# Retention, a dense MoE layer and eight routed experts on one core: weight conversion moved in time, and the expert norms one step later

## The chip, the cores and the metric

The kernel runs on one core of a Trainium2 chip. The metric is device time in microseconds (us) of one execution, the median of three runs. Engine names are those of the profile: PE (matrix engine), PEld (its weight loads), DVE (vector engine), ACT (scalar engine), POOL (GpSimd), SP (the queue from which nearly all transfers are issued).

## The reference

Three layers follow each other (float32 in and out):

```python
scores = q @ k.T / 8                 # 4 batches, 8 heads, 576 positions, 64 wide
ret = scores * D                     # D[i,j] = gamma_h ** (i-j) for i >= j, else 0
x = (ret @ v)                        # -> 2304 tokens x 512
h = x @ w_in;  g = h / (1 + exp(-1.702 h));  x = g @ w_out      # 512 -> 2048 -> 512
xn = x / (|x| + 1e-6);  en = emb / (|emb| + 1e-6)               # emb: 8 experts x 512
probs = softmax(xn @ en.T / tau);  e = argmax                   # one expert per token
out = probs[e] * (relu(x @ w1[e]) @ w2[e])                      # 512 -> 1024 -> 512
```

In this kernel the dense weights `w_in` and `w_out` come in as pairs of 32-bit words, that is as 64-bit numbers, and the chip rebuilds a float from each pair. The weights of the experts are plain floats.

## The kernel before, in words

Every product of the two feed-forward layers is made of three passes, high times high, high times low, low times high, where high is the rounded value that PE takes and low is the rest. So a weight "unit" (128 rows of the hidden layer, 1024 columns, both layers together) is a tile of a high and a low half.

**Attention** (`attention_`, L207). Sixteen pairs of heads, each of five chunks of positions, so 80 chunks; two neighbouring pairs alternate, so each pair starts five chunks after the one before. For a chunk, PE makes the scores two chunks ahead (L269, L272 for the short last chunk), DVE multiplies them by the decay table (`pr`, L274), PE makes the running state (L296), ACT copies it with a factor to `ends` (L298), and PE makes the output (L312 reads `ends`, L316 reads `pr`). POOL prepares the queries and the decayed keys of a pair two pairs ahead (`prep`, L276: L281, L284, L287). The rows of a pair are loaded into one of five buffers as soon as the pair that used it is done (`load`, L222); behind three of these loads, chosen by `WD_AT`, a dense weight unit is loaded too (L372).

**Conversion** (`convert`, L138) is a generator that issues the work for the 16 dense units, a piece at a time. For unit u: ACT takes the magnitude of the upper word (`magnitude`, L146), DVE clamps it (L159) and shifts it (L161), puts in the sign (L169) and the low bits (L171); ACT then rounds it to the high half (`high`, L149), and DVE takes the low half (`low`, L153). Each `yield` names a cost in us. ACT's two operations are not issued on the spot: they are put into `later` and issued at the next `flush()`, or when the next piece needs them. The intermediate words have two buffers, taken in turn.

**Pull** (L687) issues pieces from the list `bg` of generators until the costs reach the number given; what is overdrawn is taken off the next time. In the attention it is called after each chunk from the 53rd on with 0.36; in the dense layer once for each step. A `STOP` makes it go on with the next generator, at a charge of 0.7.

**Dense layer.** Six blocks of 384 tokens. Blocks 0 and 1 go together, unit by unit: step i is block i mod 2 with unit i // 2 (32 steps). Blocks 2 to 5 follow with 16 steps each. In step i, `dense1(i)` makes the hidden rows (PE, 12 products, L410) and the activation (`swish`, L425: ACT tanh, DVE product L434, ACT high part, then in blocks 0 and 1 `flush()` and `pull`, then DVE low part L439), and `dense2(i - 2)` adds to the outputs (PE, 9 products, L421). So the conversion of units 2 to 15 lies in the 32 steps of blocks 0 and 1, in DVE's queue between the product and the low part of each step.

**Routing.** When a block is done its outputs are copied (`evac_x`) and `dots_dve` (L500) is put into `bg`: 24 dot products of rows with the experts' vectors (L507), then `route` (L523): a chain of small DVE operations up to `oh` (L547, the chosen expert as ones and zeros), two STOPs, a PE product with `oh` that counts the places (`rk`, L554), STOP, the scatter, STOP, a store. At the end of each of the blocks 2 to 4 what is left in `bg` is issued at once (L747). `route` multiplies by `etab`, which `prep_emb` (L476) makes from the expert vectors: eight ACT squares (L479), a POOL square root (L474), three small DVE operations (L483 to L485). It is put into `bg` in step 27, after the conversion has been drained there.

**Tiles and queues.** All engines and SP work in program order. A tile of a tag with n buffers waits until the tile n before it under the same tag has been read. The tag "stg" holds the two conversion words and later `x0s`, the tokens of block 2 and on; the tag "tab" holds two of the query tiles of the attention, then the two halves of the experts' vectors (`en`), then gathered rows.

Of the kernel before, what the change touches and what calls it, by code (L numbers as in the profile page):

```python
# [13 lines left out]
I32 = mybir.dt.int32  # L14
AF = mybir.ActivationFunctionType
ALU = mybir.AluOpType

P = 128
# [5 lines left out]
KD = D // P  # L24
F1 = 2048
NF1 = F1 // P
# [13 lines left out]
WARM = 34  # L40
HOLD = NF1 - LAG - 1 - KD
STOP = 1000.0
WD_AT = (9, 12, 15)
NWD = 3
NBUF, NQ = 5, 4
HELD = NBUF + NPAIR + 4
# [16 lines left out]
def retention_moe_kernel(  # L63
# [14 lines left out]
    pool = ctx.enter_context(tc.tile_pool(name="pool", bufs=1))  # L78
# [3 lines left out]
    PE, ACT, DVE, POOL, SP = nc.tensor, nc.scalar, nc.vector, nc.gpsimd, nc.sync  # L82
# [27 lines left out]
    def new_unit(u):  # L110
        units[u] = unit_tile(f"unit{u}", [P, 2, 1024], F32R, HELD + u)
        return units[u]

    stg = {}

    def load_wd(u):

        t = unit_tile(f"wd{u}", [P, 2048], I32, HELD + u)
        stg["d", u] = t.rearrange("p (n two) -> p n two", two=2)
        SP.dma_start(t, wd[u].bitcast(I32))  # L120
# [3 lines left out]
    later = {}  # L124
    due = []

    def load_due():

        if st.get("loaded"):
            while due:  # L130
                load_wd(due.pop(0))

    def flush(*keys):
        for k in keys or list(later):
            if k in later:
                later.pop(k)()

    def convert():  # L138

        words = [pool.tile([P, 1024], I32, tag="stg", bufs=2, name=f"ca{k}") for k in range(2)]  # L140

        def word(u):
            return words[u % 2]

        def magnitude(u):
            ACT.activation(word(u).bitcast(F32), stg["d", u][:, :, 1].bitcast(F32), AF.Abs)  # L146

        def high(u):
            ACT.copy(new_unit(u)[:, 0, :], word(u).bitcast(F32))  # L149

        def low(u):
            flush(("high", u))
            DVE.tensor_tensor(units[u][:, 1, :], word(u).bitcast(F32), units[u][:, 0, :].bitcast(F32), ALU.subtract)  # L153

        magnitude(0)
        for u in range(NF1):
            a = word(u)
            flush(("mag", u))
            DVE.tensor_scalar(a.bitcast(F32), a.bitcast(F32), 2.0**-15, CLAMP_HI, ALU.max, ALU.min)  # L159
            yield 0.67  # L160
            DVE.tensor_scalar(a, a, 3, 0x3FFFFFF8, ALU.logical_shift_left, ALU.bitwise_and)  # L161
            yield 0.67
            if u:
                low(u - 1)
                yield 1.22
            if u + 1 < NF1:
                later["mag", u + 1] = lambda u=u: magnitude(u + 1)
            d = stg.pop(("d", u))
            DVE.scalar_tensor_tensor(a, d[:, :, 1], -0x40000000, a, ALU.bitwise_and, ALU.bitwise_or)  # L169
            yield 1.22  # L170
            DVE.scalar_tensor_tensor(a, d[:, :, 0], 29, a, ALU.logical_shift_right, ALU.bitwise_or)  # L171
            if u + NWD < NF1:
                due.append(u + NWD)
                load_due()
            later["high", u] = lambda u=u: high(u)
            yield 1.22
        low(u)
        yield 0.1
# [23 lines left out]
    def attention():  # L202
        psum = tc.tile_pool(name="psum_a", bufs=1, space=bass.MemoryType.PSUM, reuse_waits="tile")
        with psum as psum:
            yield from attention_(psum)

    def attention_(psum):  # L207
# [14 lines left out]
        def load(bp):  # L222
            t = row[bp % NBUF]
            b, pair = divmod(bp, NPAIR)
            if bp:
                SP.dma_start(t, att[bp])
            else:
                for j in range(2):
                    r = slice(64 * j, 64 * j + 64)
                    SP.dma_start(qz[0][r, S * j : S * j + NCH * P], att[bp, r, AQ:])  # L230
                ACT.dma_start(t[:, :AK], att[bp, :, :AK])
            if b == 0:
                SP.dma_start(tb[:, bp], tab[:, bp])
            if bp == 0:
                ACT.dma_start(t[:, AK:AQ], att[bp, :, AK:AQ])
            if pair == 0:
                SP.dma_start(tl[b % 2], tails[b])
# [121 lines left out]
        for i, (bp, ch) in enumerate(steps):  # L359
# [9 lines left out]
            if ch == NCH:  # L369
                if bp + NBUF < NBP:  # L370
                    load(bp + NBUF)
                if bp + NBUF in WD_AT:  # L372
                    load_wd(WD_AT.index(bp + NBUF))
                if bp + NBUF + 1 == NBP:
# [13 lines left out]
    def x0_tile(blk):  # L388
        return pool.tile([P, 2, KD, TB], F32R, tag="big", bufs=2, name=f"x0_{blk}")
# [7 lines left out]
    def split_x0(blk):  # L397
        x0[blk] = x0_tile(blk)
        for k in range(2):
            t = x0s.pop((blk, k))  # L400
            hi, lo = (x0[blk][:, j, 2 * k : 2 * k + 2, :] for j in range(2))
            ACT.copy(hi, t)  # L402
            (POOL if blk > 2 and k else DVE).tensor_tensor(lo, t, hi.bitcast(F32), ALU.subtract)  # L403
# [21 lines left out]
    def swish(h, name, early=False, kept=None, work=None):  # L425
        th = pool.tile([P, TB], F32, tag="th", bufs=2, name=f"{name}t")
        if kept:
            hi, lo = kept
        else:
            hi = pool.tile([P, TB], F32R, tag="g", bufs=6, name=f"{name}h")  # L430
            lo = pool.tile([P, TB], F32R, tag="g", bufs=6, name=f"{name}l")
        ACT.activation(th, h, AF.Tanh, scale=0.851)
        g = th if early else h
        DVE.scalar_tensor_tensor(g, th, 1.0, h, ALU.add, ALU.mult)  # L434
        ACT.copy(hi, g)
        if work:
            flush()
            work()
        DVE.tensor_tensor(lo, g, hi.bitcast(F32), ALU.subtract)  # L439
        return hi, lo  # L440
# [32 lines left out]
    def sqrt_(o, i):  # L473
        POOL.tensor_tensor(o, i, c[:, CHALF : CHALF + 1].to_broadcast(i.shape), ALU.pow)  # L474

    def prep_emb():  # L476
        for e in range(E):
            junk = pool.tile([P, 512], F32, tag="cvb", bufs=1, name=f"ej{e}")
            ACT.activation(junk, en[e // 4][:, e % 4, :], AF.Square, accum_out=scr[:, e : e + 1])  # L479
            yield 0.3  # L480
        nrm = small("enrm", E)
        sqrt_(nrm, scr[:, :E])
        DVE.tensor_scalar_add(nrm, nrm, 1e-6)  # L483
        DVE.tensor_scalar(nrm, nrm, scr[:, 15:16], None, ALU.mult)
        DVE.reciprocal(etab, nrm)  # L485
        yield 0.4
# [198 lines left out]
    bg, debt = [], [0.0]  # L685

    def pull(us):  # L687

        k = 0
        us += debt.pop()  # L690
        while us > 0 and k < len(bg):
            cost = next(bg[k], None)
            if cost is None:
                bg.pop(k)
            elif cost == STOP:
                k += 1
                us -= 0.7
            else:
                us -= cost
        debt.append(min(us, 0.0))  # L700

    bg.append(convert())
    for i, _ in enumerate(attention()):
        if i > 52:
            flush()
            pull(0.36)
    psum = ctx.enter_context(tc.tile_pool(name="psum", bufs=1, space=bass.MemoryType.PSUM, reuse_waits="tile"))

    def fill_slots():
# [9 lines left out]
    gs, outs = {}, {}  # L719
# [3 lines left out]
    kept = []  # L723
# [5 lines left out]
    def dense1(i):  # L729
        blk, f = steps[i]  # L730
        k = f - HOLD if blk == NB - 1 else -1
        if k == 0:
            kept.append(x0_tile("k"))
        h = layer1(f, x0[blk], TB, f"h{i}", [(dc, a, b) for dc in range(KD) for a, b in ((0, 0), (0, 1), (1, 0))])
        gs[blk, f] = swish(h, f"g{i}", blk < 3, [kept[0][:, j, k, :] for j in range(2)] if 0 <= k < KD else None, (lambda: pull(2.5)) if blk < 2 else None)

    def dense2(i):
        blk, f = steps[i]
# [111 lines left out]
    for i in range(nd - 1):  # L850
        blk, f = steps[i]
        dense1(i)
        if blk < 2:
            if f > 3:
                next(fill, None)
            if blk == 1 and f < NPAIR:
                SP.dma_start(x0d[:, f, :], x0f.pop(f))
            if (blk, f) == (1, NF1 - 3):
                while bg:
                    pull(STOP)  # L860
                load_emb()
                bg.append(prep_emb())
                load_x0(2)
            if (blk, f) == (0, NF1 - 1):
                split_x0(2)
        else:
            pull(2.6 if blk == 2 else 2.0)
            if blk < NB - 1 and f == 0:
                load_x0(blk + 1)
            if blk < NB - 1 and f == 6:  # L870
                split_x0(blk + 1)
        if i >= LAG:
            dense2(i - LAG)
            u = i - LAG - (nd - NF1)
            if u == 0:
                load_we(0)
                load_we(1)
            if 0 <= u < HOLD:
                split_we(u)
# [33 lines left out]
    for i in range(ne + LAG):  # L913
        e, f = divmod(i, NF2)
# [93 lines left out]
```

## Time and profile before

| | us |
|---|---|
| median of three runs | 794.12 (793.67 to 795.09) |
| the profiled execution | 794.88 |
| its span | 793.1 |
| PE busy | 758.5 (96%) |
| DVE busy | 455.9 (57%) |
| ACT busy | 304.4 (38%) |
| POOL busy | 225.8 (28%) |

The attention lies at 0 to 79 us of the span, blocks 0 and 1 at 79 to 230, blocks 2 to 5 to about 510, the experts behind them. In a timeline a row is the start, the duration, the engine, the line, and in brackets how long the engine had been idle and what ended that. The duration of a row of several instructions runs from the first start to the last end. DVE's rows overlap by a tenth of a us or so at their ends, so the distance from start to start is what one costs.

### The profile page before, as it was taken

To read this page: it belongs to the slowest core of one execution; us is meant where nothing else is said; L and a number is where in the kernel's file an instruction comes from. 1 tells how busy PE (TensorE), PEld (TensorE's weight loads), DVE (VectorE), ACT (ScalarE), POOL (GpSimd) and SP (SyncE) were. 2 spreads that over 40 slices of the span, in tenths; PEclk is the share of its full clock that TensorE was granted. 3 is DMA by queue.
4 is the path that set the end of the run, shared out by engine and by line. 5 is a ranking of instruction groups with operands and counts; after the bars stand their busy time and mean duration, and the time that the engine had idled before them with its cause. 6 is when DMAs were issued, how large, how long until landed. Compare 5 with 4: busy or idle time off the path is not lost.

```text
span 793.1 us, 13078 instructions
## 1 busy us (share of the span) xinstructions
PE 758.5 (96%) x4996; PEld 676.5 (85%) x4996; DVE 455.9 (57%) x1000; ACT 304.4 (38%) x572; POOL 225.8 (28%) x251
## 2 busy tenths in 40 slices
PE   7998999999799899999999998999999999999994
PEld 6987988888699799989989987888888888888883
DVE  4769777777458777753763786552543434344210
ACT  2544343444543223323322442444443534445221
POOL 4975000000002111210111223244554445544311
PEclk9999999999999999999999999999999999999998
DMA  9999995000210122012004133354554546545201
GB/s 347 330 375 324 397 388 202 1 1 1 66 40 2 48 72 81 1 37 84 1 1 134 57 117 107 113 170 151 171 179 136 177 145 184 174 162 172 80 31 35
DMA packets 31577, 104.96 MB, mean 132 GB/s; under 512 B 4495, under 2 KB 7439, under 8 KB 27280
## 3 DMA queue, kind: packets, MB, share of 16 engines
q1 hardware_dynamic: 27984, 93.78, 34.9%
q0 software_dynamic: 3232, 9.46, 3.3%
q8 instruction: 41, 0.67, 0.3%
q10 hardware_dynamic: 288, 0.79, 0.3%
q14 instruction: 32, 0.26, 0.1%
HBM read 80.88 MB, written 24.18 MB: 132 GB/s over the span
## 4 chain that ended last, share of the span: by engine, by line
PE 59%; DVE 13%; DMA 10%; issue 9%; ACT 6%; POOL 2%; SPq 0%; POOLq 0%; DVEq 0%; ACTq 0%
PE o L421 15%; PE h L410 14%; PE eo L421 11%; PE eh L410 10%; DMA wd<-wd 3%; DMA xs<-fill 3%; DVE dj L507 3%; PE sc L269 2%; DMA we<-we 2%; DVE ca L169 1%; ACT unit L149 1%; PE ao L316 1%; DMA rin<-xs 1%; ACT ca L146 1%; PE ao L312 1%
## 5 line engine op out<-in xcount | busy, mean ns | idle before, releaser
L410 PE MATMUL h<-x,unit 128*128 128x384 f32 x1152 | 221.7, 339 | 6.0 <-DVE x_k L439 2.5
L410 PEld LDWEIGHTS h<-x,unit 128*128 128x128 f32 x1152 | 203.9, 188 | 20.4 <-DVE unit L153 6.6
L190 POOL TENSOR_TENSOR unit<-we,unit 128x512 fp32r<-128x512 f32 x64 | 104.9, 1647 | 150.1 <-ACT unit L188 150.0
L410 PE MATMUL eh<-xt,unit 128*128 128x352 f32 x672 | 117.1, 323 | 0.0
L410 PEld LDWEIGHTS eh<-xt,unit 128*128 128x128 f32 x672 | 111.0, 188 | 6.3
L507 DVE CUSTOM_DVE_ANT_0 dj<-xr,en 128x512 f32<-128x512 f32 x120 | 92.8, 826 | 1.1 <-ACT xr L491 1.0
L189 DVE TENSOR_TENSOR unit<-we,unit 128x512 fp32r<-128x512 f32 x64 | 58.3, 912 | 40.8 <-ACT unit L188 40.8
L188 ACT CAST unit<-we 128x1024 fp32r<-128x1024 f32 x64 | 66.8, 1047 | 6.6 <-DMA we<-we 6.5
L269 PE MATMUL sc<-qz,row 128*64 128x128 f32 (+1 forms) x512 | 38.2, 258 | 4.0 <-POOL qz L281 1.9
L474 POOL TENSOR_TENSOR enrm<-scr,c 128x8 f32<-128x8 f32 x1 | 1.7, 1684 | 139.8 <-ACT ej L479 139.8
L274 DVE TENSOR_TENSOR pr<-sc,tb 128x256 f32<-128x256 f32 (+1 forms) x80 | 30.7, 393 | 14.5 <-PE sc L269 12.6
L451 POOL DMA_INDIRECT out<-y,idx x24 | 23.6, 982 | 49.2 <-ACT y L621 47.1
L269 PEld LDWEIGHTS sc<-qz,row 128*64 128x64 f32 x512 | 30.8, 145 | 5.6 <-POOL qz L281 2.7
L298 ACT ACTIVATE ends<-s,tb 128x64 f32<-128x64 f32 x64 | 19.8, 313 | 37.2 <-PE s L296 34.6
L153 DVE TENSOR_TENSOR unit<-ca,unit 128x1024 fp32r<-128x1024 f32 x16 | 19.6, 1228 | 21.0 <-ACT unit L149 21.0
L316 PE MATMUL ao<-pr,row 128*64 128x128 f32 x256 | 29.7, 282 | 2.1 <-DVE pr L274 2.1
L403 POOL TENSOR_TENSOR x<-x0s,x 128x768 fp32r<-128x768 f32 x3 | 6.0, 1983 | 89.3 <-ACT x L402 89.3
L451 POOL DMA_INDIRECT xs<-xr,slot x18 | 19.0, 1054 | 35.7 <-DVE ov_all L586 23.6
L296 PE MATMUL s<-row 128*64 128x64 f32 x256 | 22.5, 227 | 1.0 <-ACT ends L298 1.0
L312 PE MATMUL ao<-qz,ends 128*64 128x128 f32 x192 | 22.2, 280 | 0.8 <-issue 0.8
L316 PEld LDWEIGHTS ao<-pr,row 128*64 128x64 f32 x256 | 19.4, 141 | 3.0 <-DVE pr L274 3.0
L281 POOL COPY qz<-row 64x512 f32<-64x512 f32 x30 | 18.7, 622 | 6.0 <-PE at L312 2.8
(1258 smaller groups left out, 1523.5 us busy)
## 6 DMA issues: line engine op xcount, KB each, us to landing
we<-we SPq DMA_DIRECT2D x64, 512.0 KB, 3.5
wd<-wd SPq DMA_DIRECT2D x16, 1024.0 KB, 9.8
row<-att SPq DMA_DIRECT2D x15, 1024.0 KB, 7.7
xs<-fill SPq DMA_DIRECT2D x22, 257.0 KB, 10.8
xrow<-xr SPq DMA_DIRECT2D x18, 257.0 KB, 4.0
rin<-xs SPq DMA_DIRECT2D x8, 514.0 KB, 4.7
x0d<-x0f SPq DMA_DIRECT2D x4, 768.0 KB, 9.7
x0s<-x0d SPq DMA_DIRECT2D x8, 384.0 KB, 5.0
```

Source lines behind the costliest of these rows:

```text
L188: ACT.copy(w[:, 0, :], t)
L189: DVE.tensor_tensor(w[:, 1, :512], t[:, :512], w[:, 0, :512].bitcast(F32), ALU.subtract)
L190: POOL.tensor_tensor(w[:, 1, 512:], t[:, 512:], w[:, 0, 512:].bitcast(F32), ALU.subtract)
L269: PE.matmul(sc[64 * i : 64 * i + 64, j, q0:], t[:, k0 : k0 + 64], q[j][:, q0:P], start=True, stop=True)
L274: DVE.tensor_tensor(pr[:, :, :w], sc[:, :, :w], mask[:, :, :w], ALU.mult)
L296: PE.matmul(s[64 * j : 64 * j + 64], t[:, AK + c0 : AK + c0 + 64], t[:, AV + c0 : AV + c0 + 64], start=ch == 0, stop=True, skip_group_chec ...
L312: PE.matmul(o[64 * j : 64 * j + 64], kvs[bp % 2][:, 64 * (ch - 1) : 64 * ch], qz[bp % NQ][:, q0 : q0 + n], start=True, stop=False)
L316: PE.matmul(o[64 * j : 64 * j + 64], v, pr[:, j, :n], start=ch == 0, stop=True)
L410: PE.matmul(h, w[:, a, P * dc : P * (dc + 1)], xt[:, b, dc, :n], start=k == 0, stop=k == len(terms) - 1)
L421: PE.matmul(o, a[:, c0 : c0 + n], w[:, b, 512:], start=first and k == 0, stop=last and k == 2)
L451: i = POOL.indirect_dma_start(out=dst[:, :], out_offset=bass.IndirectOffsetOnAxis(ap=rows, axis=0), in_=src, in_offset=None, bounds_check= ...
L507: DVE.tensor_tensor_reduce(junk, r[:, :D], en[e // 4][:, e % 4, :], 1.0, 0.0, ALU.mult, ALU.add, dots[:, E * k + e : E * k + e + 1])
```

## The change

The three early loads of dense units move behind other row loads; the conversion starts behind chunk 37 with smaller pulls; from unit 3 on there are four word buffers (the third and fourth share one tile under the tag "tab"); inside a unit, the sign is put in ahead of the low half of the unit before, and the magnitude of the next unit is handed to `later` ahead of both (for unit 1 behind the low half); the pulls of blocks 0 and 1 go from 2.5 to 2.6; the experts' norms are put into `bg` in step 30 instead of step 27, with 0.9 for each square and a STOP between the square root and the small operations.

```diff
-WD_AT = (9, 12, 15)
+WD_AT = (7, 11, 14)
...
         def word(u):
-            return words[u % 2]
+
+            if u == 3 and len(words) == 2:
+                t = pool.tile([P, 2, 1024], I32, tag="tab", bufs=2, name="ca")
+                words.extend((t[:, 0, :], t[:, 1, :]))
+            return words[u % 2 if u < 3 else (2, 3, 1, 0)[(u - 3) % 4]]
...
             DVE.tensor_scalar(a, a, 3, 0x3FFFFFF8, ALU.logical_shift_left, ALU.bitwise_and)
             yield 0.67
+            d = stg.pop(("d", u))
+            if u + 1 < NF1 and u != 1:
+                later["mag", u + 1] = lambda u=u: magnitude(u + 1)
+            DVE.scalar_tensor_tensor(a, d[:, :, 1], -0x40000000, a, ALU.bitwise_and, ALU.bitwise_or)
+            yield 1.22
             if u:
                 low(u - 1)
+                if u == 1:
+                    later["mag", u + 1] = lambda u=u: magnitude(u + 1)
                 yield 1.22
-            if u + 1 < NF1:
-                later["mag", u + 1] = lambda u=u: magnitude(u + 1)
-            d = stg.pop(("d", u))
-            DVE.scalar_tensor_tensor(a, d[:, :, 1], -0x40000000, a, ALU.bitwise_and, ALU.bitwise_or)
-            yield 1.22
             DVE.scalar_tensor_tensor(a, d[:, :, 0], 29, a, ALU.logical_shift_right, ALU.bitwise_or)
...
             ACT.activation(junk, en[e // 4][:, e % 4, :], AF.Square, accum_out=scr[:, e : e + 1])
-            yield 0.3
+            yield 0.9
         nrm = small("enrm", E)
         sqrt_(nrm, scr[:, :E])
+        yield STOP
         DVE.tensor_scalar_add(nrm, nrm, 1e-6)
...
     for i, _ in enumerate(attention()):
-        if i > 52:
+        if i > 36:
             flush()
-            pull(0.36)
+            pull(0.23)
...
-        gs[blk, f] = swish(h, f"g{i}", blk < 3, [kept[0][:, j, k, :] for j in range(2)] if 0 <= k < KD else None, (lambda: pull(2.5)) if blk < 2 else None)
+        gs[blk, f] = swish(h, f"g{i}", blk < 3, [kept[0][:, j, k, :] for j in range(2)] if 0 <= k < KD else None, (lambda: pull(2.6)) if blk < 2 else None)
...
                 load_emb()
-                bg.append(prep_emb())
                 load_x0(2)
             if (blk, f) == (0, NF1 - 1):
                 split_x0(2)
+                bg.append(prep_emb())
```

## Rows read from the trace of the kernel before

**Rows 1.** The page: busy time, share of the span and instructions of each engine.

```profile
PE 758.5 (96%) x4996; PEld 676.5 (85%) x4996; DVE 455.9 (57%) x1000; ACT 304.4 (38%) x572; POOL 225.8 (28%) x251
```

**Rows 2.** Busy time by stretch, late in the attention: PE, PEld, DVE, ACT, POOL, clock, DMA.

```profile
60.00:64.00 4.00, 2.88 (x70) 2.64 (x68) 3.99 (x7) 0.94 (x3) 3.75 (x6) 1.00 0.98 365
```

**Rows 3.** Timeline of the attention: short-chunk scores of chunks 46 and 51, masks of 55 and 79.

```profile
46.59 0.29 PE L272 MATMUL sc<-qz,ends 128*64 128x64 f32 x4
50.27 0.29 PE L272 MATMUL sc<-qz,ends 128*64 128x64 f32 x4
...
55.06 0.42 DVE L274 TENSOR_TENSOR pr<-sc,tb 128x256 f32<-128x256 f32 x1 [1.67 <-PE sc L269]
...
76.91 0.28 DVE L274 TENSOR_TENSOR pr<-sc,tb 128x128 f32<-128x128 f32 x1
```

**Rows 4.** Blocks 0 and 1 in PE's timeline: the products of steps 3 and 29.

```profile
87.70 2.27 PE L410 MATMUL h<-x,unit 128*128 128x384 f32 x12
...
202.20 2.27 PE L410 MATMUL h<-x,unit 128*128 128x384 f32 x12
```

**Rows 5.** DVE's timeline in one unit of blocks 0 and 1: low half, sign, clamp.

```profile
117.72 1.23 DVE L153 TENSOR_TENSOR unit<-ca,unit 128x1024 fp32r<-128x1024 f32 x1 [1.53 <-ACT unit L149]
118.86 1.22 DVE L169 SCALAR_TENSOR_TENSOR ca<-wd,ca 128x1024 int32<-128x1024 int32 x1
...
122.63 0.69 DVE L159 TENSOR_SCALAR ca<-ca 128x1024 f32<-128x1024 f32 x1 [0.49 <-ACT ca L146]
```

**Rows 6.** Timeline around the experts' norms (step 28), then the stretch behind them.

```profile
212.99 0.17 DVE L483 TENSOR_SCALAR enrm<-enrm 128x8 f32<-128x8 f32 x1 [8.25 <-POOL enrm L474]
214.15 0.79 PE L421 MATMUL o<-unit,g28l 128*128 128x512 f32 x1 [5.28 <-DVE g28l L439]
217.61 2.27 PE L410 MATMUL h<-x,unit 128*128 128x384 f32 x12
...
214.15:217.20 3.05, 3.05 (x7) 2.47 (x8) 1.90 (x4) 1.91 (x4) 0.00 (x0) 0.50 0.00 0
```

**Rows 7.** PE's timeline in block 2: products of steps 41 and 43, the place count between.

```profile
259.48 2.27 PE L410 MATMUL h<-x,unit 128*128 128x384 f32 x12
264.26 0.17 PE L554 MATMUL rk<-oh_all,ub 128*128 128x24 bf16 x1 [2.52 <-DVE dots L507]
...
272.26 2.27 PE L410 MATMUL h<-x,unit 128*128 128x384 f32 x12
```

**Rows 8.** Transfers: row loads 10 to 12, a weight unit's landing, all weight units' landings.

```profile
35.93 8.23 SPq L226 DMA_DIRECT2D row<-att  x3
...
wd<-wd SPq DMA_DIRECT2D x1, 1024.0 KB, 9.2
...
DMA to landing us min/median/max: 6.0/9.8/15.8
```

**Rows 9.** ACT's timeline in the attention: the magnitude of unit 1.

```profile
58.66 1.15 ACT L146 ACTIVATE ca<-wd 128x1024 f32<-128x1024 f32 x1
```

**Rows 10.** POOL's timeline: the decayed keys of two pairs, before and under the conversion.

```profile
53.12 1.04 POOL L284 TENSOR_TENSOR row<-row,tb 128x512 f32<-128x512 f32 x1
...
63.18 2.13 POOL L284 TENSOR_TENSOR row<-row,tb 128x512 f32<-128x512 f32 x1
```

**Rows 11.** Timeline at the end of block 2: last dot products, route of block 1, place count.

```profile
293.50 0.69 DVE L507 CUSTOM_DVE_ANT_0 dj<-xr,en 128x512 f32<-128x512 f32 x1
...
295.41 0.14 DVE L507 DVE_READ_ACCUMULATOR2_ANT dots<- 128x1 f32 x1
...
297.66 0.16 DVE L534 TENSOR_SCALAR ss<-ss 128x3 f32<-128x3 f32 x1
...
299.36 0.18 DVE L547 TENSOR_TENSOR oh_all<-cand,fst 128x24 bf16<-128x24 f32 x1
...
301.37 0.56 DVE L439 TENSOR_TENSOR g49l<-h,g49h 128x384 fp32r<-128x384 f32 x1 [0.55 <-ACT g49h L435]
301.57 0.19 PE L554 MATMUL rk<-oh_all,ub 128*128 128x24 bf16 x1
```

## The prediction, made before the changed kernel was run

> **What bounds the kernel now.** I read the busy shares first: PE is busy 96% of the span and no other engine comes near [rows 1], so only an edit that closes a gap of PE, or opens one, moves the time. Next the busy time by stretches, for where PE falls short: late in the attention DVE is full (3.99 of 4 us) and POOL nearly, while PE has 2.88 [rows 2]. Then the waits and the timelines of the two dense stretches. The undisturbed step of the dense layer comes from PE's products of step 31 (217.61) and step 41 (259.48): 41.87 us for ten steps, 4.187 each [rows 6, 7]. Against it, the 26 steps from step 3 to step 29 of blocks 0 and 1 take 114.50 instead of 108.86 [rows 4]: 5.6 us too long. There DVE sets the pace: in every unit it stands 1.53 us for ACT's high half and 0.49 us for ACT's magnitude [rows 5]. Step 28 holds one long stop [rows 6], and block 2 another, at the place count of block 0's routing [rows 7].
>
> **The change part by part.** All sums stand against the profiled execution, 794.88 us; the median is 0.76 below it, and I take that off at the end.
>
> *Experts' norms.* DVE stood 8.25 us for POOL's square root, which stood behind eight ACT squares, and the low part of step 28 was queued behind that wait; PE lost 5.28 us waiting for it [rows 6]. [...] From step 29 (202.20) to step 31 (217.61) it took 15.41 us where two steps are 8.37 [rows 4, 6]: 7.0 lost. With the change the squares are issued in the pulls of steps 31, 32 and 33 (three, three, two, at 0.9 against 2.6), the square root in step 33, and the DVE operations, behind the STOP, in step 34. A step lies between, so nothing waits; ACT has to fit three squares and three copies of outputs into steps 32 and 33, and its delay is covered by the two steps that lie between a step's activation and its use on PE. If that cover failed, DVE would be late by a us or two in block 2. Removed: 7.0 (bounds 5.3, if only the wait goes, and 7.0).
>
> *Conversion in blocks 0 and 1.* I counted the pieces off by their costs: each pull issues pieces while the sum so far is under the budget (9.89 from the attention plus 2.6 a step, formerly 9.72 plus 2.5). Before, the low bits of a unit fell into the pull just before that of its low half, so ACT's high half was issued right when DVE needed it: hence the 1.53. With the new order the low bits of unit f (3 and on) are issued two pulls ahead of its low half, or more, and its high half one step (4.19 us) before it is wanted; the magnitude, free of the old word buffer, is also issued a step ahead of its clamp. So 2.02 us of waits a unit go, against 0.43 that PE lost a unit (5.6 over 13): PE is next late by nothing, as DVE's work in two steps, 8.8 less 2.0, is 1.6 us under PE's 8.37. The start is worse: in step 0's pull the sign of unit 2 now stands ahead of the low half of unit 1, and PE's step 2 waits for that; one sign is 1.14 us from start to start [rows 5]. A few tenths more in the first steps, where a magnitude is still just in time: 0.3, an estimate. Net removed: 5.6 - 1.4 = 4.2 (bounds: 0, if ACT is late anyhow, and 5.6).
>
> *Attention.* Five chunks take PE 3.68 us (46.59 to 50.27), 0.736 a chunk; from chunk 55 to chunk 79, under the conversion, 24 chunks take 21.85 instead of 17.66 [rows 3]: 4.2 lost. The same pieces (two units and the start of a third) now lie over 43 chunks instead of 27. DVE's full 3.99 of 4 then becomes about nine tenths, but a piece of 1.1 us still pushes a mask back: I keep 1.2 us of the 4.2 as lost (bounds 0 and 4.2). Against that stands a new wait. The magnitude of unit 1 is issued to ACT behind chunk 43, which by the tail scores is at 46.6 [rows 3]. Its words are now loaded behind row load 11, the middle one of three between 35.93 and 44.2, so at about 40.2; a weight unit issued right behind a row landed after 9.2 us [rows 8], here at 49.4. ACT then stands 2.8 us and takes 1.15 [rows 9]; queued behind it are the state copies of chunk 44 and on, which PE needs in chunk 46, about 2.4 us after 46.6 with the conversion's own delay. PE loses about 2.0 (bounds: 0 if it lands after 6.0; 8.4 if after 15.8, the extremes of all 16 [rows 8]). Net removed: 4.2 - 1.2 - 2.0 = 1.0.
>
> [...] POOL's keys took 1.04 us alone and 2.13 beside DVE's conversion [rows 10]. [...]
>
> *Routing of block 0.* It starts a step later and two steps later reaches its place count. The stop there (step 41 to step 43 took 12.78 us instead of 8.37, so 4.4, of which 2.52 is the wait [rows 7]) comes from DVE being late with dot products queued ahead. DVE's load in those steps stays the same, so I leave it: 0 (bounds: 4.4 less, and 1.5 more).
>
> *Routing of block 1.* This is given back. With the later start, the last dot product and the front of `route` for block 1 fall into the pull of step 49, and the drain at the end of block 2 issues the place count directly behind it; before, the front was a step earlier and PE found `oh` ready at 301.57. The new order on DVE: low part of step 49 until 301.93, one dot product of 0.64 (three from 293.50 to 295.41), the front 1.88 (297.66 to the end of `oh`), so `oh` at 304.45: PE waits 2.9 us [rows 11]. Afterwards the clock: behind the two stops above the loss was 1.8 and 1.9 beyond the wait [rows 6, 7]. Added: 2.9 + 1.8 = 4.7 (bounds 0 and 5).
>
> *The rest at nothing.* The second half of the experts' vectors now waits for the last conversion word, and the loads of block 2's tokens stand behind it on SP; they are wanted some 12 us later. The remaining dense units are loaded as before.
>
> Sum: -7.0 - 4.2 - 1.0 + 0 + 4.7 = -7.5, that is 787.4 for the profiled kind of execution and **786.6** against the median.
>
> **The rivals.**
> 1. *The place count of block 1 costs nothing*, because DVE runs ahead at the end of block 2 or my count of the pieces is off by one: 786.6 - 4.7 = 781.9. For it: the budget and the pieces come within one dot product of each other there. Against: the drain issues count and front in one go. If the attention's 4.2 goes whole as well, 779. Chance 0.2.
> 2. *The conversion does not gain.* DVE stays the pace of blocks 0 and 1, because four buffers only move the wait from ACT's high half to something else: 786.6 + 4.2 = 790.8. Against: ACT's two operations of a unit and those of its two steps fill well under 8.4 us. Chance 0.1.
> 3. *POOL becomes the bound in the attention.* If each conversion piece blocks POOL, POOL's work for a pair no longer fits into five chunks, 3.68 us. The key product went up by 1.09 [rows 10] under pieces that lay 1.6 times as dense (43 chunks against 27), so about 0.7 a pair now. Two pairs from chunk 37 on still have POOL's low parts of block 0 and 1 tokens (L345) and no room, the later ones have: 1.4 more, 788.0 (bounds 0 and 9.9, all 1.15 us of pieces in each of 8.6 pairs). For it: POOL's 3.75 of 4 in [rows 2]. Against: POOL prepares two pairs ahead. Chance 0.15.
> 4. *Slower than before*: the words of unit 1 land very late. ACT's magnitude then holds the state copies, and PE stands in chunk 46 until they land. Each us past 49.4 is a us; at 15.8 us, the longest of the 16 [rows 8], 6.6 more and 1.8 for the clock: 795.0. It decides from a landing of about 15 us on. For it: row, words and tails share a queue that is 0.98 full [rows 2]. Against: the unit that was issued in the like place took 9.2. Chance 0.06.
>
> **How the numbers follow.** The forecast itself gets 0.45, rivals 1 to 4 0.2, 0.1, 0.15 and 0.06; 0.04 is left for what I don't see, on the slower side. The bounds above leave 780.0 to 791.5 as the range for 8 times in 10. A measurement of this kernel can't tell a difference under 0.2%, 1.6 us. Faster by more than that: 0.87; within it: 0.06 (rival 2 with more given back, or half of rival 4); slower: 0.07.
>
> **What would show it.** DVE's wait for POOL at L483 gone, and PE's products of steps 29 to 31 at 4.19 us. DVE's waits for L149 and L146 gone from unit 3 on, and steps 3 to 29 in about 109 us. The first product of step 2 delayed by a us more. ACT idle for a transfer before its second L146, near 47. A wait of PE for `oh` at the place count at the end of block 2, of about 2.9 us, with a clock of about 0.5 behind it. The prediction is wrong if that last wait is absent, if PE still waits for L153 in every unit, or if the attention ends later than now.

## The result and the profile after

The changed kernel took 785.74 us in the median (four executions, 785.15 to 788.28) against 794.61 of the kernel before beside it (793.67 to 795.50): a ratio of 0.9895, with an interval of 0.987 to 0.992. Forecast were 786.6. The profiled execution was the longest of the four, 788.28, with a span of 786.4; a later experiment shows where a second profiled execution of the same kernel is shorter.

The page after; PE lost 1.8 us of busy time and 6.7 us of span (compare [rows 1]):

```profile
PE 756.7 (96%) x4996; PEld 678.1 (86%) x4996; DVE 458.3 (58%) x1000; ACT 306.6 (39%) x572; POOL 226.6 (29%) x251
```

PE's timeline after, for [rows 4, 6, 7, 11]: the start, steps 3, 29 and 31, then block 2 around its two place counts.

```profile
85.06 2.03 PE L416 MATMUL h<-x,unit 128*128 128x384 f32 x10 [1.01 <-DVE unit L157]
...
89.02 1.23 PE L416 MATMUL h<-x,unit 128*128 128x384 f32 x6
...
197.88 2.27 PE L416 MATMUL h<-x,unit 128*128 128x384 f32 x12
...
206.25 1.05 PE L416 MATMUL h<-x,unit 128*128 128x384 f32 x5
...
256.49 2.27 PE L416 MATMUL h<-x,unit 128*128 128x384 f32 x12
...
260.85 0.17 PE L561 MATMUL rk<-oh_all,ub 128*128 128x24 bf16 x1 [2.09 <-DVE dots L514]
...
268.85 2.27 PE L416 MATMUL h<-x,unit 128*128 128x384 f32 x12
...
285.60 2.27 PE L416 MATMUL h<-x,unit 128*128 128x384 f32 x12
...
292.62 0.18 PE L561 MATMUL rk<-oh_all,ub 128*128 128x24 bf16 x1 [2.67 <-DVE oh_all L554]
...
292.72 4.19 PE L416 MATMUL h<-x,unit 128*128 128x384 f32 x12
...
299.74 2.27 PE L416 MATMUL h<-x,unit 128*128 128x384 f32 x12
```

From step 3 (89.02) to step 29 (197.88) it is 108.86 us, exactly 26 steps of 4.187, where it was 114.50; from step 29 to step 31 (206.25) it is 8.37 instead of 15.41. Two steps are 8.37, so the place count of block 0 cost 3.99 (268.85 less 256.49, less 8.37) and that of block 1 cost 5.77 (299.74 less 285.60, less 8.37). The products at 292.72 take 4.19 instead of 2.27: the clock. The windows behind the two counts (PE, clock, DMA) show it at 0.57 and 0.50:

```profile
261.00:265.00 4.00, 4.00 (x15) 0.57 0.00 0
292.70:296.90 4.20, 4.20 (x17) 0.50 0.41 148
```

DVE in one unit of blocks 0 and 1, for [rows 5]: here the low half and the clamp come without a wait for ACT, where the one stood 1.53 us and the other 0.49. Not every unit is like this one: between steps 3 and 29 DVE's waits for ACT's two operations of the conversion fell from 26.3 us to 6.9, and in five of the later units the clamp still stands about 0.49. PE loses nothing to them.

```profile
121.69 1.22 DVE L157 TENSOR_TENSOR unit<-ca,unit 128x1024 fp32r<-128x1024 f32 x1
...
125.88 0.69 DVE L163 TENSOR_SCALAR ca<-ca 128x1024 f32<-128x1024 f32 x1
```

The attention after, for [rows 3, 9]: PE's short-chunk scores of chunks 41, 46 and 79, a stop and the first dense products; then ACT's magnitude of unit 1 with its wait for the words.

```profile
43.02 0.29 PE L278 MATMUL sc<-qz,ends 128*64 128x64 f32 x4
...
47.78 0.28 PE L278 MATMUL sc<-qz,ends 128*64 128x64 f32 x4
...
50.29 0.34 PE L318 MATMUL at<-qz,ends 128*64 128x64 f32 x4 [0.23 <-ACT ends L304]
...
76.83 0.29 PE L278 MATMUL sc<-qz,ends 128*64 128x64 f32 x4
...
79.27 4.78 PE L416 MATMUL h<-x,unit 128*128 128x384 f32 x26 [0.31 <-DVE x0f L340]
```

```profile
48.84 1.20 ACT L150 ACTIVATE ca<-wd 128x1024 f32<-128x1024 f32 x1 [0.62 <-DMA wd<-wd]
```

The same scores of chunks 41 and 79, and the first dense products, in the kernel before:

```profile
42.90 0.29 PE L272 MATMUL sc<-qz,ends 128*64 128x64 f32 x4
...
75.61 0.29 PE L272 MATMUL sc<-qz,ends 128*64 128x64 f32 x4
...
79.11 1.14 PE L410 MATMUL h<-x,unit 128*128 128x384 f32 x5 [0.31 <-DVE x0f L334]
```

38 chunks at the undisturbed 0.736 are 28.0 us. From the one score to the other it took 33.8, and 32.7 before; behind the last one it is 2.4 us to the first dense product instead of 3.5. One execution of each kernel doesn't settle what the change did here, but the profiled executions below hold the same attention several times. Four have it as before (the kernel before, and three runs below without this edit), seven as in the changed kernel (three more runs below alter it further and are left out):

| profiled executions | score of chunk 41 to score of chunk 79 | from there to the first dense product | first dense product |
|---|---|---|---|
| four, attention as before | 32.71 to 34.22, mean 33.4 | 3.5 | 79.11 to 80.89, mean 80.0 |
| seven, with the edit | 33.05 to 33.87, mean 33.5 | 2.4 | 78.48 to 79.27, mean 78.8 |

So the edit leaves the 38 chunks as they were and wins 1.05 us behind them. There PE stood 0.35 us for a mask and 0.52 for a state copy in the kernel before, both behind a conversion piece, and for neither in the changed kernel. The kernel before was the earliest of its four, the changed kernel the latest of its seven: that is why the two starts shown differ by only 0.16, the wrong way. (One of the expectations below calls the two scores those of chunks 39 and 77, by the chunk during which they are issued.)

### The profile page after: what moved, and what is told of

Its sections match the earlier page's. It is cut to its first block, busy times and chain, and to the rows that moved or that the text cites. A ratio compares the mean times of both kernels' runs of the same rounds, so it can differ in the third digit from the quotient of the medians.

```text
span 786.4 us, 13066 instructions
## 1 busy us (share of the span) xinstructions
PE 756.7 (96%) x4996; PEld 678.1 (86%) x4996; DVE 458.3 (58%) x1000; ACT 306.6 (39%) x572; POOL 226.6 (29%) x251
## 4 chain that ended last, share of the span: by engine, by line
PE 73%; DVE 10%; issue 8%; ACT 4%; DMA 3%; POOL 2%; SPq 0%; POOLq 0%; ACTq 0%; DVEq 0%
PE h L416 20%; PE o L427 20%; PE eo L427 12%; PE eh L416 12%; DVE dj L514 4%; PE sc L275 2%; PE ao L322 2%; PE ao L318 1%; DMA row<-att 1%; PE tp L619 1%; DMA we<-we 1%; PE s L302 1%; DVE unit L195 1%; POOL out L457 1%; POOL unit L196 1%
## 5 line engine op out<-in xcount | busy, mean ns | idle before, releaser
L514 DVE CUSTOM_DVE_ANT_0 dj<-xr,en 128x512 f32<-128x512 f32 x120 | 91.2, 813 | 0.0
L304 ACT ACTIVATE ends<-s,tb 128x64 f32<-128x64 f32 x64 | 19.7, 312 | 33.0 <-PE s L302 30.5
L572 POOL TENSOR_TENSOR cum<-cum,oh_all 128x8 bf16<-128x8 bf16 x18 | 3.6, 202 | 62.4 <-PE rk L565 61.5
```

The source lines that it names most:

```text
L514: DVE.tensor_tensor_reduce(junk, r[:, :D], en[e // 4][:, e % 4, :], 1.0, 0.0, ALU.mult, ALU.add, dots[:, E * k + e : E * k + e + 1])
```

## The experiments

Each run was timed beside the kernel before, whose median was 794.3 to 795.5 us in the four groups of runs; the ratios, with their 95% intervals in brackets, are against it. The runs of the same kernel scatter by some us, so a difference between two variants counts only where their intervals part.

### Which edit earned it

**Norms alone**, on the kernel before:

```diff
-            yield 0.3
+            yield 0.9
         sqrt_(nrm, scr[:, :E])
+        yield STOP
...
                 load_emb()
-                bg.append(prep_emb())
...
                 split_x0(2)
+                bg.append(prep_emb())
```

> The kernel before with the norms' edit alone (put into the list in step 30, 0.9 a square, STOP behind the root). Theory A, each edit acts where it stands: steps 29 to 31 lose their 7.0 us of stop and slow clock, and the later start of the routing alone moves block 1's place count to directly behind the front of its chain, which gives back 5.6: about 1.8 us under the kernel before, 792.8. Steps 3 to 29 stay at 114.5. Theory B, the new wait at the place count comes from another of the edits (buffers, pulls): no wait of PE over 1 us for the ones and zeros at the end of block 2, and 7 us under, 787.6.

788.94 (786.45 to 791.59), ratio 0.992 [0.9895, 0.9945]. Steps 29 to 31 took 8.37, so 7.0 are gone; the new wait at block 1's place count is there, so theory A has the mechanism. PE at the two counts:

```profile
265.35 0.17 PE L555 MATMUL rk<-oh_all,ub 128*128 128x24 bf16 x1 [1.44 <-DVE dots L508]
...
295.56 0.17 PE L555 MATMUL rk<-oh_all,ub 128*128 128x24 bf16 x1 [2.67 <-DVE oh_all L548]
...
295.66 2.36 PE L410 MATMUL h<-x,unit 128*128 128x384 f32 x12
```

But the products behind the wait take 2.36, not 4.19: the granted clock was 1.00 (from 296 to 300), and the place count cost 3.0 in all (the products of steps 49 and 51 start at 288.54 and 299.94) instead of 5.8. And block 0's count, which theory A left alone, cost 1.8 (two steps across it take 10.15) instead of 4.4: a wait of 1.44 instead of 2.52, and a clock of 1.00 behind it (from 264.5 to 268.5) instead of 0.63 (from 264.2 to 268.2 in the kernel before). These 2.8 and 2.6 us are more than the 4 by which the time came out under theory A; PE was late by 0.9 from the attention in this execution.

**Conversion alone** (the new order, the four buffers, 2.6; norms and attention as before):

> The kernel before with the new order inside a unit, four word buffers and pulls of 2.6 in blocks 0 and 1, the norms and the attention as before. Theory A: steps 3 to 29 give 5.6 us, the start loses 1.2, the stop at the norms in step 28 stays: 790.2. Theory B, the conversion's gain is worth having only with the norms out of the way, because DVE arrives at step 28 with the same wait and all is lost again there: 793 to 795, with DVE's wait for POOL still at 8 us and the steps 29 to 31 longer than the 15.4 of before.

785.67 (783.74 to 789.98), ratio 0.9886 [0.9859, 0.9913]: on its own as fast as the whole change within the intervals, and better than both theories. The stop at the norms is still there, but PE waits 1.98 instead of 5.28 us, the clock is 1.00 from 206 to 210, and the step (202.81 to 209.25) loses 2.25. PE and DVE around it:

```profile
207.30 0.51 PE L427 MATMUL o<-unit,g28l 128*128 128x512 f32 x1 [1.98 <-DVE g28l L445]
```

```profile
197.33 0.55 DVE L440 SCALAR_TENSOR_TENSOR g28t<-g28t,h 128x384 f32<-128x384 f32 x1 [2.22 <-ACT g28t L438]
...
206.13 0.17 DVE L489 TENSOR_SCALAR enrm<-enrm 128x8 f32<-128x8 f32 x1 [8.25 <-POOL enrm L480]
```

DVE waits the same 8.25 us as in [rows 6]. What differs is when that begins. Here the products of step 28 end at 196.7, and DVE takes up their activation 0.6 us later. In the kernel before they end at 200.3, but ACT comes to its part only at 202.45, behind the high half of unit 15, for which DVE was late, and DVE to its own only at 204.19, behind the low half of that unit. That is 3.9 us:

```profile
198.26 2.02 PE L410 MATMUL h<-x,unit 128*128 128x384 f32 x10 [0.20 <-DVE unit L153]
...
201.50 1.05 ACT L149 CAST unit<-ca 128x1024 fp32r<-128x1024 f32 x1 [0.68 <-DVE ca L171]
202.45 0.48 ACT L432 ACTIVATE g28t<-h 128x384 f32<-128x384 f32 x1
...
204.19 0.55 DVE L434 SCALAR_TENSOR_TENSOR g28t<-g28t,h 128x384 f32<-128x384 f32 x1
```

So 3.3 us of the old stop (3.9 less 0.6, and 5.28 less 1.98) was the conversion's lateness. Behind the 1.98 that are left the next products take their 2.27 us, here and in the run below.

**The changed kernel without the norms' edit:**

> The changed kernel with the norms' edit undone (list entry in step 27, 0.3 a square, no STOP), the conversion's and the attention's edits kept. Theory A, the new order of the conversion alone already shortens the stop at the norms from 7.0 to 2.3 us, so the norms' edit is worth 2.3 there and gives back 2.9 at block 1's place count: steps 28 to 29 take 6.4 us, no wait of 2.7 at the place count, and the same time as the changed kernel within 1 us, 784 to 785.5. Theory B, the norms' edit is worth its 7.0 us less the 2.9 given back: 788 to 790.

783.85 (782.75 to 787.52), ratio 0.9874 [0.9848, 0.9901]: theory A in the trace, and a time just under A's range and far from B's. The stop at the norms is the one of 2 us, its step takes 6.43, and there is no wait at block 1's place count:

```profile
205.72 0.50 PE L427 MATMUL o<-unit,g28l 128*128 128x512 f32 x1 [1.98 <-DVE g28l L445]
```

**Attention alone** (loads behind rows 7, 11 and 14; from chunk 37 with 0.23):

> The kernel before with the attention's edit alone (loads behind rows 7, 11 and 14, conversion from chunk 37 on with pulls of 0.23). Theory A, spreading the pieces saves nothing because the loss goes by their number and not by their density: the products of step 0 start within 0.5 us of the 79.1 of before, total 794 to 795. Theory B (the prediction's): the conversion's loss shrinks by 3 us and what was lost in the full change is a wait that the other edits brought: start at 76 to 78, total 792 to 793.5.

793.97 (792.65 to 795.07, 12 executions), ratio 0.9981 [0.9968, 0.9995], so 0.4 to 2.5 us won. The time lies between the theories; in the trace the scores of chunks 41 and 79 lie 33.05 apart (before 32.7) and the first dense product starts at 78.82, so spreading shortens nothing there, as A says. The gain is the 1.05 us behind the last score.

### The place counts and the clock

**The changed kernel once more:**

> The changed kernel once more, unaltered, for a second profiled execution. In the first one the granted clock fell to about half behind the two place counts of block 2, which took 1.6 and 2.9 us beyond the waits themselves; behind stops of the same length in three other kernels it did not fall. Theory A, whether it falls there differs from execution to execution: the waits are again about 2.1 and 2.7, steps 48 to 50 take 11.4 instead of 14.1 in this profile, and its span is 783 to 784.5, as in the three unprofiled runs. Theory B, the fall belongs to this kernel: 14.1 us again and a span of 786.

784.38 (783.40 to 784.48), ratio 0.9871 [0.9854, 0.9888], span 781.6: theory A. The waits are the same to 0.01 us, and nothing follows them:

```profile
260.44 0.17 PE L561 MATMUL rk<-oh_all,ub 128*128 128x24 bf16 x1 [2.08 <-DVE dots L514]
...
290.64 0.17 PE L561 MATMUL rk<-oh_all,ub 128*128 128x24 bf16 x1 [2.66 <-DVE oh_all L554]
...
290.74 2.33 PE L416 MATMUL h<-x,unit 128*128 128x384 f32 x12
```

```profile
290.90:295.00 4.10, 4.10 (x22) 3.71 (x23) 2.18 (x15) 2.00 (x5) 2.65 (x5) 1.00 0.42 160
```

Of the 4.8 us between the two spans, 4.3 lie in these two places: two steps across them take 10.80 and 11.37 us here, 12.36 and 14.14 in the first execution.

**Block 2 with larger pulls**, 2.75 for 2.6:

> The changed kernel with pulls of 2.75 instead of 2.6 in block 2, so that by the count of pieces the front of block 1's routing is issued a step before the place count. Theory A: the wait of 2.67 us at that count and the slow clock behind it go, steps 49 to 51 take 8.4 to 8.6 us instead of 14.1: 5.6 us under the changed kernel, 780. Theory B, DVE is full in block 2 and 0.15 a step more makes it late elsewhere: the wait moves to another step (the low parts of steps 42 to 48), and the time stays at 784 to 787.

782.89 (781.61 to 785.38), ratio 0.9849 [0.9824, 0.9874]. The wait at block 1's place count is gone, as in A:

```profile
257.51 0.17 PE L561 MATMUL rk<-oh_all,ub 128*128 128x24 bf16 x1 [3.41 <-DVE dots L514]
...
289.08 0.19 PE L561 MATMUL rk<-oh_all,ub 128*128 128x24 bf16 x1
```

The gain over the changed kernel is 1.5 to 2.9 us by the medians, not 5.6, and the intervals overlap. The clock's part is not always there to be won, as the run before shows, and the wait at block 0's count grew from 2.1 to 3.4: a part of the wait moved to another place, as theory B has it, though not to the low parts.

**Norms spread, but put into the list in step 27 again:**

```diff
                 load_emb()
+                bg.append(prep_emb())
...
                 split_x0(2)
-                bg.append(prep_emb())
```

> The changed kernel with the norms put into the list in step 27 again, as before, but still with 0.9 a square and the STOP behind the root. Theory A, only the spreading and the STOP are needed against the stop at the norms, and putting the list entry later is what delays the routing by a step: no stop at steps 28 to 31, the front of block 1's routing a step before the place count, no wait over 0.5 us there, and 2.9 us under the changed kernel, 782.8. Theory B, the squares in steps 28 to 30 delay ACT's high halves and tanh: a stop of 1 to 2 us at steps 28 to 31, total 784 to 786.

783.77 (782.42 to 784.83), ratio 0.9867 [0.9849, 0.9885]. In the trace all that A says holds: steps 28 to 31 at 4.19, 49 to 51 at 8.58. The gain over the changed kernel is 0.6 to 2.0 us, below A's 2.9, and its interval overlaps that of the changed kernel. The stop at block 0's count is still there (PE waits 2.5).

### The attention

**No conversion in it** (all of its pieces issued in one go behind the attention):

> The changed kernel with the pieces of the conversion that lay in the attention issued in one go behind it, loads of the words where they are. Theory A, the conversion's pieces are what stretches the attention: the short-chunk scores of chunk 39 and chunk 77 lie 28 to 29 us apart instead of 33.8, whether the pieces act by DVE's queue or by POOL. Theory B, the loads of the words between the rows, or POOL's own 93 percent, stretch it: 31 us or more. Behind the attention PE then stands for the conversion, so the total rises, by 2 to 6 us.

793.96 (one execution). PE's timeline: the scores of chunks 41 and 79, and every stop that it names in between.

```profile
42.91 0.29 PE L278 MATMUL sc<-qz,ends 128*64 128x64 f32 x4
...
48.51 0.44 PE L318 MATMUL ao<-qz,ends 128*64 128x128 f32 x4 [0.62 <-issue]
...
54.95 0.27 PE L318 MATMUL ao<-qz,ends 128*64 128x128 f32 x1 [0.86 <-issue]
...
61.22 0.44 PE L275 MATMUL sc<-qz,row 128*64 128x128 f32 x6 [0.65 <-issue]
...
67.28 0.44 PE L275 MATMUL sc<-qz,row 128*64 128x64 f32 x5 [0.59 <-issue]
...
74.49 0.22 PE L278 MATMUL sc<-qz,ends 128*64 128x64 f32 x1
```

31.6 us, so theory B: with no conversion at all 3.6 us beyond the undisturbed 28.0 are still lost, where the kernel before lost 4.7. In four places some 6.2 us apart, 2.7 us in all, PE stands for nothing that these views name ("issue"), at 54.95 in the middle of a group of four. The total rose by 8 us or more, beyond the 2 to 6 expected.

**In addition the words behind the last row load:**

> The previous kernel without conversion in the attention, and in addition the words of the first three dense units loaded only behind the last row load (issued at about 57 us) instead of between the rows. Without conversion the 38 chunks from the short scores at 42.9 still took 31.6 us where the undisturbed pace gives 28.0, and PE stood 3.1 us of it for nothing that the profile names, in stretches where the transfers' share was about 1.0. Theory A, the words between the rows are what does it: the 38 chunks take 28 to 29.2 us and PE's unnamed stops there fall under 1 us in sum. Theory B, the stops come with the program's own length or with the rows alone: 31 us or more again, with stops every 6 us. The total is about that of the kernel before or above (the conversion starts late), and says nothing here.

789.41 (one execution). From score to score it is 31.0, with three such stops:

```profile
42.81 0.31 PE L278 MATMUL sc<-qz,ends 128*64 128x64 f32 x3
...
54.03 0.27 PE L318 MATMUL ao<-qz,ends 128*64 128x128 f32 x1 [0.58 <-issue]
...
65.71 0.44 PE L275 MATMUL sc<-qz,row 128*64 128x64 f32 x5 [0.86 <-issue]
...
71.88 0.27 PE L302 MATMUL s<-row 128*64 128x64 f32 x1 [0.69 <-issue]
...
73.83 0.22 PE L278 MATMUL sc<-qz,ends 128*64 128x64 f32 x1
```

Theory A falls: 3.0 us are still lost, 2.1 of them in these stops. The stops near 48.5 and 61 went and one near 72 came, where the words were now loaded. B had two readings, the program's own length and the rows. The first agrees with the packed traces, which also hold the start and the duration of every transfer of the queue that the page calls "instruction" (q8, 41 transfers of 16 KB). For the four stops of the run before this one:

| transfer ends (us) | PE goes on | later by | records of PE and PEld before that |
|---|---|---|---|
| 47.08 | 48.51 | 1.43 | 1729 |
| 53.55 | 54.95 | 1.40 | 1985 |
| 59.83 | 61.22 | 1.39 | 2241 |
| 65.87 | 67.28 | 1.41 | 2497 |

The counts lie 256 apart each time. The three stops here fit as well (1.31, 1.36 and 1.36 behind a transfer, at 1985, 2497 and 2753). So each of these stops goes with a transfer and with a place in the program. What PE stands for there isn't shown, since no run moved those transfers by themselves, and neither is why the stops come in some executions and not in others.

**Copies of the query tails on ACT instead of POOL:**

```diff
-                POOL.tensor_copy(qz[bp % NQ][r, q0 : q0 + TAIL], end[r])
+                ACT.copy(qz[bp % NQ][r, q0 : q0 + TAIL], end[r])
```

> The changed kernel with the two small copies per pair that fill the last 64 columns of the queries moved from POOL to ACT, 0.74 us of POOL's 3.7 a pair. Theory A, in the attention POOL is the bound under the conversion (no idle time between 41 and 69 us): the 38 chunks from 43 us on take 29 to 31 us instead of 33.8, the products of step 0 start 3 to 5 us earlier, total 781 to 783. Theory B, the bound is DVE, whose masks stand behind conversion pieces: the start moves by less than 1 us, total 785 to 786.5 (above, if the copies on ACT hold up the state copies).

786.10 (785.14 to 788.21), ratio 0.9893 [0.9877, 0.9909]: the total says B, the trace neither. From score to score (45.78 to 77.21) it took 31.4, less than in any of the seven executions above. But ACT held up state copies, since the copies that now stood ahead of them waited 1.75 and 2.19 us for the load of the tails, and PE lost 2.7 us ahead of that stretch:

```profile
22.75 0.34 PE L302 MATMUL s<-row 128*64 128x64 f32 x4 [1.07 <-ACT ends L304]
...
39.36 0.34 PE L302 MATMUL s<-row 128*64 128x64 f32 x4 [1.65 <-ACT ends L304]
...
45.78 0.28 PE L278 MATMUL sc<-qz,ends 128*64 128x64 f32 x4
...
77.21 0.29 PE L278 MATMUL sc<-qz,ends 128*64 128x64 f32 x4
```

That POOL is the bound under the conversion is not shown by it. In the second execution of the changed kernel POOL waited 2.2 us between the same scores, for a row load and for PE, and they lay 33.75 apart all the same; and in neither execution does a wait of PE there end with POOL. Besides POOL's work, three things differ here: the stretch begins some 3 us later, so that what is prepared ahead had that much more time; DVE's 63 operations in it are busy 28.2 us where they took 29.2 to 30.5 in the seven; and there is no unnamed stop. But two of the seven have no such stop either, and took 33.2 and 33.6. Which of the other things gave the 2 us was not separated.

### A version that beats both

Norms early and spread, 2.75, and two more edits: no dot products between the front of block 0's routing and its place count, and for unit 2 the low half of unit 1 ahead of the sign.

```diff
-        yield STOP
+        yield STOP if t0 else 3.0
...
+            if u == 2:
+                low(1)
+                yield 1.22
             DVE.scalar_tensor_tensor(a, d[:, :, 1], -0x40000000, a, ALU.bitwise_and, ALU.bitwise_or)
             yield 1.22
-            if u:
+            if u and u != 2:
```

> The changed kernel with the norms spread but put into the list in step 27, pulls of 2.75 in block 2, no dot products in the pull between the front of block 0's routing and its place count, and in the first steps the low half of unit 1 ahead of the sign of unit 2. Theory A, the two remaining stops go (2.9 us at the place count of block 0, 1.2 us in step 1): 4 us under the kernel with the spread norms, 779.7. Theory B, DVE is late at the place count because block 2 gives it too much work, and not because dot products stand ahead in that one pull: PE still stands 1.5 us or more there, total 782 to 784.

780.45 (779.38 to 780.65), ratio 0.9809 [0.9791, 0.9826]: theory A, and clear of the changed kernel's intervals. All that PE waits for between 79 and 320 us:

```profile
PE o L430 <- DVE g3l L448: 0.4, 1, 0.4
PE h L419 <- DVE x0f L343: 0.3, 1, 0.3
PE h L419 <- DVE unit L157: 0.2, 1, 0.2
```

**The same with the attention's edit undone:**

> The previous kernel with the attention's edit undone (words behind rows 9, 12 and 15, conversion from chunk 53 on with pulls of 0.36). Theory A, the attention's edit is worth 0.7 to 1.5 us as it was alone on the kernel before: 780.4 to 781.2. Theory B, it was worth something only beside the old order of the conversion: the same time as the previous kernel within 0.5 us.

780.10 (779.37 to 782.01), ratio 0.981 [0.9792, 0.9828]: by the timed runs theory B, but the interval of 0.0018 either way is 1.4 us and can't tell A's 0.7 to 1.5 from nothing. In the two profiled executions the first dense product started at 78.80 with the edit and 80.89 without.

## Why the prediction was right, and where not

The time was right, 786.6 against 785.7 and, in the other group of runs, 784.4. It was right in part by luck: the attention's term came out of two wrong parts, and the clock behind block 1's count differs from execution to execution. The terms, in the profiled execution and where another run has them:

| step of the prediction | forecast | measured |
|---|---|---|
| norms | -7.0 | -7.04 |
| conversion, steps 3 to 29 | -5.6 | -5.64 |
| conversion, start | +1.4 | +1.16 |
| attention | -1.0 | +0.16 (here); -1.2 between the means of seven and four; -1.5 [-2.5, -0.4] alone |
| place count, block 0 | 0 | -0.42; -1.98 the second time |
| place count, block 1 | +4.7 | +5.56; +2.8 the second time |

**Norms.** The sum is right and the reason is only half of it. I took the whole of the stop for the norms' own. Conversion alone shows that 4.8 of its 7.0 us go with DVE's lateness, which belongs to another edit. Beside that edit the norms' edit is worth 2.3 us at its place and gives 2.8 back at block 1's count, or 5.6 where the clock falls, so it brings nothing that can be measured: 783.85 without it. The table hides that, since both edits were made.

**Conversion.** Right for PE: 4.187 over all 26 steps, and one sign (forecast 1.4 with the few tenths, measured 1.16: step 3 starts 9.75 us behind the first dense product instead of 8.59) lost at the start. For DVE it was right in the main only: of 26.3 us of waits 19.4 went, not all, and what is left fits into the slack that PE's pace leaves to DVE.

**Attention.** The step that failed, though its sum came out (-1.2 in the means for -1.0). First, the wait for unit 1's words: I had them land at 49.4, with ACT ready for them at 46.6. They landed at 48.84, and ACT was ready only at 48.22, since PE's chunks were themselves later (47.78 for the score that stood at 46.59 in [rows 3]). ACT stood 0.62, and PE lost 0.23, not 2.0. Second, of "4.2 lost under the conversion" the thinner spread was to save 3.0, and it saved nothing: 33.5 us from score to score in the mean with it, 33.4 without. With no conversion at all (one execution of each of two runs) 3.0 to 3.6 us are lost, 2.1 to 2.7 of them in unnamed stops, so that the conversion itself adds some 2 to the 28.0. I had compared a late stretch with an undisturbed early one and put the whole difference down to the one thing that I knew was new in it. What was won, 1.05 us behind the last short score, is in none of my terms. My sign of being wrong, an attention that ends later than now, is met by the two executions of the result (79.27 for 79.11), and not by the means.

**POOL, the third rival.** It was forecast at 1.4 us, and stays open. With less work for POOL some 2 us went, but not by that alone, as said there. What the traces do show is the stretching of some of its operations: of the eight key products from 40.78 to 67.14 in the changed kernel five took 1.04 us, two 1.36 and 1.37, and the one at 52.90, beside DVE's low bits (52.36, 1.53 us), 1.90. That each conversion piece blocks POOL is not shown, nor that PE loses by the stretching.

**Place count of block 1.** The order on DVE came as worked out: the wait 2.67 for a forecast of 2.9. The term's second part, the clock at 1.8, is not one number: 3.1 us beyond the wait in one execution of the changed kernel, 0.3 in the other.

Of the other rivals, the first (no cost at block 1's count), the second (no gain from the order) and the fourth (words so late that the change loses) are each refuted by a row above.

## What to carry to other kernels

Two stops that lie one behind the other in a queue are not two terms: ask of each what it would be once the other is gone, and price an edit on the version that holds the rest of the change. An edit that makes a chain start later is to be followed to the chain's last reader; here that reader sat behind a fixed drain, and a step's delay became 2.8 us, more with the clock. And before a slow stretch is put down to what is new in it, run it without that, and see first how far several executions of one kernel differ there: the attention of the kernel before took 32.7 to 34.2 us over the same 38 chunks.

## What the runs showed of the hardware

The clock falls behind some stops and not behind others that look the same. In twelve profiled executions PE stood 1.4 to 3.4 us at a place count 18 times. Behind seven of these the granted clock went to 0.50 to 0.68 in the mean of the next 3 us, and the place cost 1.7 to 3.1 us beyond the wait; behind eleven it stayed at 1.00, and it cost 0.3 to 0.4 beyond. Where an execution had two such stops, it fell behind both or neither, and for one and the same kernel it fell in one execution and not in the next. Behind the two stops of 5.3 us it fell both times, to 0.50. So what such a short stop costs beyond its wait is a range from 0.3 to 3.1 us here, and one profile doesn't give it.

PE's unnamed stops in the attention are 0.2 to 1.2 us long: 23 of them in eleven of the fourteen profiled executions, and none in the other three. Every one ends 1.26 to 1.53 us after the end of a 16 KB transfer of the queue that the page calls "instruction", and in PE's own order every one comes behind the same count of records of PE and PEld, 1217 or that and a multiple of 256. So one lay in the same place of the program in several variants (before its products at 54.07, 54.95 and 54.03 in three of them, each behind 1985). The timeline calls them "issue"; what PE stands for in them was not shown. In the run without conversion they were 2.7 of the 3.6 us lost. What brings such a stop in one execution and not in another was not tested. In the two runs without conversion, a change of when the words were loaded also changed which of the stops came.
